# Fused attention and gated attention experts: the sum of the gate weights on GpSimd in place of VectorE, and the instructions in another order

## The chip, the cores and the metric

The kernel runs on one core of a Trainium2 chip. The metric is the device time of one launch in microseconds (us), the median over the runs of a kernel. The core's engines each work through a queue of their own, in order: TensorE (PE in the profile) for matrix products, ScalarE (ACT) for tanh and exp, VectorE (DVE), GpSimd (POOL), and SyncE (SP), which issues the transfers. PEld in the profile is TensorE's loading of weights, which may lie beside its products. Semaphores make one engine wait for another.

## The reference

Two layers in one launch. The first is attention with a soft cap, for 8 batches and 12 heads, 448 positions and 64 channels a head; the second is a gated attention with four experts, of which two count for each position.

```python
# layer 1: q, k, v of (8, 12, 448, 64)
scores = q @ k.T / sqrt(64)
scores = cap * tanh(scores / cap)          # cap = 30
attn = softmax(scores)
x = (attn @ v).transpose(0, 2, 1, 3).reshape(8, 448, 768)
# layer 2: w_gate (768, 4); wq, wk, wv (4, 768, 64); wo (4, 64, 768)
logits = x @ w_gate
topk = the two largest of four
w = softmax over the two chosen logits
for e in range(4):
    q, k, v = x @ wq[e], x @ wk[e], x @ wv[e]
    a = softmax(causal(q @ k.T / 8))
    ye = a @ v @ wo[e]
    out += (w of e where e is among the two, else 0) * ye
```

The output is (8, 448, 768) in float32.

## The kernel before, in words

**Layer 1** goes by pairs of heads: 48 pairs, six to a batch. For a pair, the float32 inputs are loaded by SyncE, cast to 16 bits on GpSimd (`cast`: k in L623, the zero-padded k in L628, q in L638, tails of k and v in L659 and L669, v in L664), transposed on TensorE (`tr`, L678 and L688) and copied out of PSUM on VectorE to `qk` (L707, L715). `fill` has TensorE write the scores into two PSUM regions, X and Y: `heads` (L752) and `tails` (L762), which are the last 64 keys. ScalarE makes three tanh of each pair (L805: Y1, X, Y2, where X holds 1344 columns and Y 896), and one exp of all of them (L817, 3136 columns for most pairs, 2240 for narrower ones). `pv` multiplies by v in two halves (L832 the tails, L839 the rest; a column of ones gives the sums). VectorE takes the reciprocal of the sums (`rca`, L860) and scales into `xk` (L863), which also sets the PSUM bank free. `xt` transposes `xk` on TensorE with a permutation (L878, `perm` and `pswap`), and VectorE copies that to `xT` (L887).

**Layer 2** follows a batch behind. `b_v` and `b_qk` project xT on TensorE (L947, L974); the logits of the gate come out of the same products as v. The gate is a chain of small tensors of 128 partitions, with four positions a partition:

- `b_gate` (GpSimd, L1014 to L1027): compares the logits pairwise and finds the ranks; `ms[0]`, `ms[1]` mark the first and the second expert
- `b_gate1` (GpSimd, L1036 to L1042): the difference of the two logits, in `g_e`
- `b_gexp` (GpSimd, L1048): its exponential, as a power of e
- `b_gate2`: 1 + e (VectorE, L1056), its reciprocal (VectorE, L1057), and on GpSimd e times that (L1058) and the two masked weights `mw` (L1060)

`b_mask` spreads the marks over the channels (`mB`, GpSimd, L1069), transposes them (L1080) and multiplies them into the queries (`qm`, VectorE, L1085 or L992). `b_score` (L1113) writes the scores of the chosen expert into the X region, in a batch twice, once for each rank; ScalarE's exp of them (L1122, 1024 columns) stands between the tanhs and exps of layer 1; `causal` zeroes what is masked, on GpSimd (L1132, L1139). `b_pv` multiplies by v (L1172), VectorE scales by the reciprocal of the sum and by `mw` (`oB`, L1187), `b_ot` adds the two ranks on GpSimd (`oS`, L1197) and transposes, `b_wo` multiplies by wo (L1234), in eight halves of 384 columns. `evac` (L381) copies each out of PSUM to `ob`, on VectorE or, near the end, on ScalarE, and SyncE stores it. The last batch is finished by `last2` and `last`.

**The order.** Every instruction is recorded as an operation with an occupancy and a latency, then `solve` builds the queues in one pass: of the operations of an engine that can start, it takes the one with the earliest due time. The activations of layer 1 and the exps of layer 2 on ScalarE are one fixed chain (`act(..., fixed=True)`). Due times are worked back from that chain. Operations with no score behind them get a due time by hand: that of the `xT` copy is `ACTS["Y1", p]` plus an offset, that of an `ob` copy another. What is taken depends on small numbers as well: a floor for due times, a bonus for operations in a PSUM group that is open, a tolerance for the start (`near`), a look ahead for operations marked `first`, and `SEEDS`, one number for each window of 4 us of planned time, which scatters the due times in it by up to half of `JIT` to either side. The costs in these calls (0.11, lat 0.17 and so on) steer the plan alone; the chip starts each instruction when its engine reaches it and its semaphores are there.

```python
d = u.due + lag if u.first or left < TAIL else max(u.due + lag, t0 + 1.12)
d -= 0.211 * (u.grp is not None and not u.opens and left >= TAIL)
k = SEEDS[int(t0 / 4.0)] if t0 < 4.0 * len(SEEDS) else 0
if k:
    d += ((u.idx * 40503 + k * 9973) % 1009 / 1009.0 - 0.5) * JIT
```

Of the kernel before, what the change touches and what calls it, by code (L numbers as in the profile page):

```python
# [11 lines left out]
ALU = mybir.AluOpType  # L12
# [4 lines left out]
SWITCH = 0.1  # L17
WARM = 5.5
TAIL = 4
LAND = 1.95  # L20
FLIGHT = 8
JIT = 0.549
SEEDS = (0, 277, 719, 88, 790, 157, 709, 606, 285, 730, 63, 826, 999, 577, 0, 998, 560, 424, 0, 0, 0, 0, 0, 618, 784, 951, 0, 460, 25, 911, 435, 331, 710, 235, 192, 243, 759, 815, 762, 59, 135, 842, 518, 725, 260, 0, 0, 0, 737, 833, 0, 852, 0, 951, 0, 877, 795, 0, 495, 199, 407, 374, 655, 0, 288, 645, 0, 0, 872, 410, 701, 204, 988, 494, 733, 571, 666, 645)
TWIRE = 0.1
BEGIN = {"POOL": 0.8, "DVE": 0.9, "SP": 0.8, "ACT": 0.8, "PE": 1.25}
NWARM = 9
# [25 lines left out]
class Graph:  # L52
# [79 lines left out]
    def solve(self, when, banks, lent):  # L132
        free = dict(BEGIN)
        sent = []
        ready = {}
        at = {}
        bank_at = {b: 0.0 for b in (*banks, *lent)}
        taken = {b: [o for o in self.ops if b in o.takes] for b in lent}
        for o in self.ops:
            o.nd = len(o.deps)  # L140
            if o.grp is not None:
                o.grp.bank = None
            if o.nd == 0:
                ready.setdefault(o.eng, []).append(o)
                at[o.idx] = 0.0
        order = []
        n = len(self.ops)
        left = sum(o.fixed for o in self.ops)
        half = 0
        lag = 0.0  # L150
        wire = 0.0

        def pick(o, t):
            best = None
            for b in o.grp.banks:
                s = max(t, bank_at[b])
                if s >= INF:
                    continue
                if b in taken and taken[b]:
                    continue  # L160
                if best is None or s < best[0]:
                    best = (s, b)
            return best or (INF, None)

        def est(o, e):
            t = max(free.get(e, 0.0), at[o.idx])
            if o.opens:
                t = pick(o, t)[0]
            for b in o.takes:
                t = max(t, bank_at[b])  # L170
            if (e == "SP" or o.wire) and len(sent) >= FLIGHT:
                t = max(t, sent[-FLIGHT])
            if e == "PE" and o.half != half:
                t = max(t, free.get(e, 0.0) + SWITCH)
            return t

        while len(order) < n:
            best = None
            for e, rs in ready.items():
                if not rs:  # L180
                    continue
                c = [(est(o, e), o) for o in rs if e == o.eng or not left]
                if not c:
                    continue
                t0 = min(x[0] for x in c)
                if t0 >= INF or (best is not None and t0 >= best[0]):
                    continue
                def rank(x):
                    u = x[1]
                    if u.name[:4] == "gexp":  # L190
                        return -INF, 0.0, 0
                    d = u.due + lag if u.first or left < TAIL else max(u.due + lag, t0 + 1.12)
                    d -= 0.211 * (u.grp is not None and not u.opens and left >= TAIL)
                    k = SEEDS[int(t0 / 4.0)] if t0 < 4.0 * len(SEEDS) else 0
                    if k:
                        d += ((u.idx * 40503 + k * 9973) % 1009 / 1009.0 - 0.5) * JIT
                    return d - 2.0 * (u.half == 1 and half == 1), u.due, u.idx

                near = t0 + (0.003 if left >= TAIL else SWITCH + 0.02)
                t, o = min((x for x in c if x[0] <= near), key=rank)  # L200
                early = e == "POOL" and t < HEAD
                if (e in ("PE", "DVE") or early) and not o.first:
                    for t2, u in c:
                        if u.first and u.due + lag < t + o.occ + 0.047 and t2 < t + (
                                o.occ if early else max(SWITCH + 0.01, min(o.occ, 0.25))):
                            t, o = t2, u
                            break
                if best is None or t < best[0]:
                    best = (t, e, o)
            assert best is not None, "stuck"  # L210
            t, e, o = best
            ready[o.eng].remove(o)
            if o.alt:
                ready[o.alt[0]].remove(o)
                if e != o.eng:
                    o.eng, o.occ, o.lat = o.alt
            left -= o.fixed
            o.start = t
            if e == "PE" and t < WARM:
                o.lat = 2.0 * o.base  # L220
                free[e] = t + 2.0 * o.base
                o.lat += 0.165
            else:
                free[e] = t + o.occ
            if o.wire:
                wire = max(wire, t + LAND) + o.wire
                o.lat = wire - t + 0.35
            if o.eng == "SP" or o.wire:
                sent.append(t + o.lat)
            if e == "PE":  # L230
                half = o.half
            if o.idx in when:
                lag = t - when[o.idx]
            if o.opens:
                b = pick(o, t)[1]
                o.grp.bank = b
                bank_at[b] = INF
            for b in o.takes:
                bank_at[b] = INF
                if b in taken:  # L240
                    taken[b].remove(o)
            if o.closes:
                bank_at[o.grp.bank] = t + o.lat + SEM
            for b in o.frees:
                bank_at[b] = t + o.lat + SEM
            order.append(o)
            for s, late in o.succ:
                at[s.idx] = max(at.get(s.idx, 0.0), t + self.gap(o, s, late))
                s.nd -= 1
                if s.nd == 0:  # L250
                    ready.setdefault(s.eng, []).append(s)
                    if s.alt:
                        ready.setdefault(s.alt[0], []).append(s)
        return order
# [19 lines left out]
def kernel(  # L274
# [13 lines left out]
    nc = tc.nc  # L288
# [12 lines left out]
    W1 = 320  # L301
# [4 lines left out]
    LB = B - 1  # L306
# [60 lines left out]
    def dve(occ, fn, r=(), w=(), grp=None, due=None, name="", lat=None):  # L367
        return G.op("DVE", occ, fn, r, w, occ + 0.085 if lat is None else lat, due, grp, name=name)
# [22 lines left out]
    def turned(n, dst, src, r, w, name, due=None):  # L391
# [58 lines left out]
    gt2 = [sb(f"gt2_{i}", sh, f32) for i, sh in enumerate(  # L450
        ([128, 1, E], [128, 1, E], [128, 1, E, E], [128, 2, 1, 1]))]
# [544 lines left out]
    def g_(b, fn, r, w, occ, lat):  # L996
        gp(occ, fn, r, [(b, y) for y in w], lat=lat, name=f"g{b}")
# [47 lines left out]
    def b_gexp(b, m=4):  # L1045
        x = b % 2
        e = g_e[x][:, 0:m]
        g_(b, lambda: nc.gpsimd.tensor_tensor(e, eul[:, 0:m], e, ALU.pow), [(b, "e"), "eul"],  # L1048
           ["e"], 1.05, 1.18)

    def b_gate2(b, m=4):
        x = b % 2
        V = nc.vector
        w = slice(0, m)
        e, w0 = g_e[x][:, w], g_w0[x][:, w]
        dve(0.11, lambda: V.tensor_scalar_add(w0, e, 1.0), [(b, "e")], [(b, "w0")], lat=0.17)  # L1056
        dve(0.1, lambda: V.reciprocal(w0, w0), [(b, "w0")], [(b, "w0")], lat=0.18)  # L1057
        g_(b, lambda: nc.gpsimd.tensor_tensor(e, e, w0, ALU.mult), [(b, "w0")], ["e"], 0.15, 0.28)  # L1058
        for s, t in ((0, w0), (1, e)):
            g_(b, lambda s=s, t=t: nc.gpsimd.tensor_tensor(  # L1060
                mw[s][x][:, w], ms[s][x][:, w], t.broadcast_to((128, m, E)), ALU.mult),
                [(b, f"ms{s}"), (b, "w0" if s == 0 else "e")], [f"mw{s}"], 0.17, 0.3)
# [404 lines left out]
    def last2(ref):  # L1467
# [63 lines left out]
        for e in range(E):  # L1531
            pe(0, lambda e=e: pv_(e), [("p2", e), "vL"] + [("vB", x, c) for c in range(3)],
               [("pvL", 3)], g, occ=0.12, name="pvL3")
        normed(3, g, view, ("pvL", 3), (gt2[0].rearrange("p o e -> p e o"), [(b, 2, "z"), (b, 2, "s")]),
               gt2[3][:, 1, 0], W1, (ref, 9.679))

# [12 lines left out]
    for p in range(NPV):  # L1551
# [13 lines left out]
        for what in order:  # L1565
            if what == "Y2" and p:
# [1 line left out]
                if p in exps:  # L1568
                    b_score(*exps[p])
                pv(p - 1)  # L1570
                xt(p - 1, (ACTS["Y1", p], 4.601))
                if p % HP == 0 and p < NP:
                    bb = p // HP - 1
                    b_v(bb, ACTS["Y1", p])
# [13 lines left out]
                if p in exps:  # L1588
                    bb, s = exps[p]
                    b_pv(bb, s)  # L1590
                    if s == 1:
                        b_ot(bb)
                        b_wo(bb, ACTS["Y1", p], *((14.83, 1.8) if bb < LB - 1 else (10.566, 0.5)))
            fill(p, what)
            tanh(p, what)
            if 0 < p < KEEP:
# [66 lines left out]
```

## Time and profile before

| | |
|---|---|
| median of 3 runs | 309.87 us (309.51 to 310.26) |
| the profiled execution | 309.16 us |
| its span in the profile | 307.4 us, 1.76 us less than its time |
| granted TensorE clock | 0.991 of full speed |
| busy: TensorE, ScalarE | 280.5 us (91%), 290.8 us (95%) |
| busy: VectorE, GpSimd | 216.0 us (70%), 181.4 us (59%) |
| HBM traffic over the span | 154 GB/s |

How to read it: busy time counts an instruction from its start to its end, and on ScalarE an activation that has been started but whose input isn't there yet counts as busy as well; the distance between the starts of two neighbours tells more than the duration. In rows of the timeline the columns are the start in us, the length in us, the engine, the line, the operation, what it writes and reads, shape and count; in square brackets stands idle time before it and what ended it. In rows of groups, behind the bar stand the busy time in us and the mean of one in ns, then idle time and its releaser. In rows of waits the columns are the sum in us, the number and the longest.

The chain of work that ended last runs over TensorE for 53% of the span, ScalarE for 30%, VectorE for 8% and GpSimd for 5%.

### The profile page before, as it was taken

How to read it: one execution, taken by the hardware profiler on the slowest of the kernel's cores; microseconds unless marked ns; L12 is line 12 of the kernel's file. 1: busy time of each engine (PE TensorE's matmuls, PEld its weight loads, DVE VectorE, ACT ScalarE, POOL GpSimd, SP SyncE). 2: the span in 40 equal slices, each digit the busy share in tenths (PEclk: the TensorE clock that was granted, in tenths of full speed). 3: DMA queues.
4: the chain of work that ended last, by engine and by line, in shares of the span. 5: the costliest groups of instructions: out<-in, count | busy, mean ns of one | idle time of the engine just before them, and what ended most of it. 6: DMA issues, size and time to landing. Idle time of an engine off the chain costs nothing.

```text
span 307.4 us, 8998 instructions
## 1 busy us (share of the span) xinstructions
PE 280.5 (91%) x3504; PEld 188.2 (61%) x3504; DVE 216.0 (70%) x660; ACT 290.8 (95%) x245; POOL 181.4 (59%) x502
## 2 busy tenths in 40 slices
PE   8787679999999999999999999999999989999992
PEld 4454446576655766667566676567665766577761
DVE  2363656477679867796866887787768765787882
ACT  3999999999999999999999999999999999999671
POOL 7883436499788572984649873946585413720320
PEclk9997999999999999999999999999999999999998
DMA  6997999899991798249975593186127600422136
GB/s 168 263 213 178 271 277 257 235 238 243 252 240 47 224 265 234 69 130 269 250 195 135 149 320 95 43 248 175 18 43 163 159 8 20 122 72 79 34 144 217
DMA packets 82075, 51.98 MB, mean 169 GB/s; under 512 B 42736, under 2 KB 78320, under 8 KB 82032
## 3 DMA queue, kind: packets, MB, share of 16 engines
q1 hardware_dynamic: 81728, 51.18, 63.7%
q8 instruction: 27, 0.44, 0.6%
q10 hardware_dynamic: 304, 0.23, 0.2%
q14 instruction: 16, 0.13, 0.1%
HBM read 36.19 MB, written 11.01 MB: 154 GB/s over the span
## 4 chain that ended last, share of the span: by engine, by line
PE 53%; ACT 30%; DVE 8%; POOL 5%; issue 2%; DMA 1%; DVEq 0%; ACTq 0%; POOLq 0%
ACT yp L805 15%; ACT yp L817 12%; PE A L974 7%; PE A L839 6%; PE Y L752 6%; PE A L947 4%; PE X L1113 4%; PE A L1234 4%; PE A L832 3%; PE A L1172 2%; PE A L878 2%; PE A L678 2%; DVE ob L381 2%; ACT pP L1122 2%; PE X L762 2%
## 5 line engine op out<-in xcount | busy, mean ns | idle before, releaser
L817 ACT ACTIVATE yp<-yp 128x3136 f16<-128x3136 f16 (+4 forms) x51 | 139.8, 2744 | 0.0
L805 ACT ACTIVATE yp<-Y 128x896 f16<-128x896 f32 (+2 forms) x100 | 96.2, 962 | 1.6 <-PE Y L752 1.6
L805 ACT ACTIVATE yp<-X 128x1344 f16<-128x1344 f32 (+2 forms) x50 | 65.9, 1318 | 0.1
L839 PE MATMUL A<-v,yp 128*128 128x65 f16 x1116 | 55.9, 194 | 0.0
L839 PEld LDWEIGHTS <-yp 128*128 128x128 f16 x1116 | 49.0, 98 | 4.9 <-issue 2.9
L832 PE MATMUL A<-vtz,yp 128*128 128x130 f16 x186 | 41.5, 223 | 10.0 <-ACT yp L817 5.4
L863 DVE TENSOR_TENSOR xk<-A,rca 128x256 f16<-128x256 f32 (+1 forms) x96 | 39.7, 415 | 2.8
L860 DVE RECIPROCAL rca<-A 128x4 f32<-128x4 f32 (+1 forms) x96 | 17.2, 179 | 25.6 <-PE A L839 24.1
L638 POOL CAST q<-qf 112x512 f16<-112x512 f32 x44 | 26.6, 613 | 13.6 <-DMA qf<-in_q_dram 6.6
L664 POOL CAST v<-vf 128x384 f16<-128x384 f32 x48 | 24.4, 514 | 11.2 <-PE A L839 7.1
L381 DVE COPY ob<-A 128x384 f32<-128x384 f32 (+1 forms) x52 | 28.1, 552 | 3.9 <-PE A L1234 2.8
L832 PEld LDWEIGHTS <-yp 128*128 128x128 f16 x186 | 18.1, 97 | 20.0 <-ACT yp L817 11.2
L1187 DVE SCALAR_TENSOR_TENSOR oB<-A,rcb,mw 128x256 f16<-128x256 f32 x54 | 25.3, 479 | 1.4
L715 DVE COPY qk<-A 128x960 f16<-128x960 f16 x33 | 21.0, 653 | 7.2 <-PE A L678 6.7
L752 PE MATMUL Y<-qk 64*128 64x448 f16 x136 | 24.9, 361 | 0.8 <-ACT yp L805 0.4
L1234 PE MATMUL A<-wo,oT 128*128 128x384 f16 x108 | 24.3, 326 | 0.8 <-DVE ob L381 0.3
L1197 POOL TENSOR_TENSOR oS<-oB,oB 128x512 f16<-128x512 f16 x14 | 16.1, 1153 | 14.4 <-DVE oB L1187 10.4
L1172 PE MATMUL A<-vB,pP 128*128 128x260 f16 x135 | 22.8, 274 | 1.0 <-DVE qk L715 0.7
L947 PE MATMUL A<-wvg,xT 128*128 128x260 f16 x168 | 23.0, 274 | 0.2
L678 PE MATMUL A<-ident,q 112*128 112x112 f16 x192 | 20.2, 212 | 2.3 <-DVE q L638 0.8
L623 POOL CAST k<-kf 128x384 f16<-128x384 f32 x33 | 16.6, 512 | 9.7 <-DMA kf<-in_k_dram 6.0
L887 DVE COPY xT<-A 128x448 f16<-128x448 f16 (+1 forms) x48 | 18.0, 377 | 4.8 <-PE A L878 4.5
(231 smaller groups left out, 587.3 us busy)
## 6 DMA issues: line engine op xcount, KB each, us to landing
qf<-in_q_dram SPq DMA_DIRECT2D x23, 448.0 KB, 6.3
kf<-in_k_dram SPq DMA_DIRECT2D x23, 384.0 KB, 5.7
vf<-in_v_dram SPq DMA_DIRECT2D x23, 384.0 KB, 5.1
out_dram<-ob SPq DMA_DIRECT2D x21, 384.0 KB, 3.3
ktf<-in_k_dram SPq DMA_DIRECT2D x46, 32.0 KB, 5.0
vtf<-in_v_dram SPq DMA_DIRECT2D x46, 32.0 KB, 4.5
out_dram<-ob SPq DMA_DIRECT2D x6, 192.0 KB, 3.3
ob<-in_moe_wv_dram SPq DMA_DIRECT2D x2, 384.0 KB, 5.0
```

What stands on the lines that cost most here:

```text
L381: (nc.scalar.copy if o.eng == "ACT" else nc.vector.tensor_copy)(dst(), src())
L638: e(q16[i], qf[s][:, h].rearrange("p h (c d) -> p c h d", c=QC))
L678: nc.tensor.transpose(ps[:, 0:S].rearrange("m (g c t) -> m c g t", c=QC, t=16)[:, c], q16[i][:, c, :, :].rearrange("p h d -> p (h d)"), id ...
L752: nc.tensor.matmul(dst[:, g, o], kT[r, 128 * (c + 1) : 128 * (c + 2)], t[r, qs], start=True, stop=True,)
L805: ACTS[what, p] = act(c_act(n * (b - a)), lambda: nc.scalar.activation(y[:, a:b, 0:n], src[:, 0 : b - a, 0:n], AF.Tanh, scale=isc / capf), ...
L817: act(c_act(n * (b - a), False), lambda a=a, b=b, n=n: nc.scalar.activation(y[:, a:b, 0:n], y[:, a:b, 0:n], AF.Exp, scale=capf), ks, ks, f ...
L832: nc.tensor.matmul(ps[:, n, :, :], y[:, 2, w : w + 128], vtz[u], start=(n == 0), stop=False, skip_group_check=True,)
L839: nc.tensor.matmul(ps[:, n, h, :], y[:, SLOT[c][h], w : w + 128], v16[u][:, h, c, :], start=False, stop=(c == 2), skip_group_check=True,)
L863: dve(c_dve(128 * m), lambda g=g, i=i, rc=rc, m=m: nc.vector.tensor_tensor(xk[p % NXK][:, 2 * i : 2 * i + m, :, :], view(g)[:, 0:m, :, 0:D ...
L947: nc.tensor.matmul(bank(g)[:, 0 : E * Dh + E], xT[x][:, j, w : w + 128], wvg[:, j, :], start=(j == 0), stop=(j == NDC - 1),)
L1172: nc.tensor.matmul(bank(g)[:, 0 : E * (Dh + 1)], pB[pi][:, o : o + 128], vB[x][:, c, :, :], start=(t == 0), stop=(t == len(cs) - 1),)
L1234: nc.tensor.matmul(bank(g)[:, 0 : D // 2], oT[x][:, n // 2, r, n % 2, :], wo2[r][:, c0:c1], start=(r == 0), stop=(r == 1),)
```

## The change

The addition of 1 to e leaves `b_gate2`, where VectorE did it (`V.tensor_scalar_add`, L1056). In `b_gexp` GpSimd does the same addition behind the power, with an instruction of its own (`tensor_scalar` with `ALU.add`). VectorE's reciprocal then reads what GpSimd wrote. There is one such addition a batch in seven of the eight batches. Beside that, 50 of the 78 numbers in `SEEDS` differ, as do the floor for due times, the bonus, the tolerance, the look ahead, and three offsets of due times. No other operation is added or removed, but the queues stand in another order, and near the end some copies out of PSUM are made by the other of ScalarE and VectorE. In the kernel after, the lines behind `b_gexp` have numbers higher by one.

```diff
--- before.py
+++ after.py
@@ -20,7 +20,7 @@
 LAND = 1.95
 FLIGHT = 8
 JIT = 0.549
-SEEDS = (0, 277, 719, 88, 790, 157, 709, 606, 285, 730, 63, 826, 999, 577, 0, 998,
...
+SEEDS = (0, 0, 719, 88, 733, 597, 709, 0, 78, 526, 63, 826, 0, 653, 0, 128,
...
 TWIRE = 0.1
 BEGIN = {"POOL": 0.8, "DVE": 0.9, "SP": 0.8, "ACT": 0.8, "PE": 1.25}
 NWARM = 9
@@ -189,19 +189,19 @@
                     u = x[1]
                     if u.name[:4] == "gexp":
                         return -INF, 0.0, 0
-                    d = u.due + lag if u.first or left < TAIL else max(u.due + lag, t0 + 1.12)
-                    d -= 0.211 * (u.grp is not None and not u.opens and left >= TAIL)
+                    d = u.due + lag if u.first or left < TAIL else max(u.due + lag, t0 + 1.124)
+                    d -= 0.191 * (u.grp is not None and not u.opens and left >= TAIL)
                     k = SEEDS[int(t0 / 4.0)] if t0 < 4.0 * len(SEEDS) else 0
                     if k:
                         d += ((u.idx * 40503 + k * 9973) % 1009 / 1009.0 - 0.5) * JIT
                     return d - 2.0 * (u.half == 1 and half == 1), u.due, u.idx
 
-                near = t0 + (0.003 if left >= TAIL else SWITCH + 0.02)
+                near = t0 + (0.012 if left >= TAIL else SWITCH + 0.02)
                 t, o = min((x for x in c if x[0] <= near), key=rank)
                 early = e == "POOL" and t < HEAD
                 if (e in ("PE", "DVE") or early) and not o.first:
                     for t2, u in c:
-                        if u.first and u.due + lag < t + o.occ + 0.047 and t2 < t + (
+                        if u.first and u.due + lag < t + o.occ + 0.0 and t2 < t + (
                                 o.occ if early else max(SWITCH + 0.01, min(o.occ, 0.25))):
                             t, o = t2, u
                             break
@@ -1047,13 +1047,14 @@
         e = g_e[x][:, 0:m]
         g_(b, lambda: nc.gpsimd.tensor_tensor(e, eul[:, 0:m], e, ALU.pow), [(b, "e"), "eul"],
            ["e"], 1.05, 1.18)
+        g_(b, lambda: nc.gpsimd.tensor_scalar(g_w0[x][:, 0:m], e, 1.0, None, ALU.add), [(b, "e")],
+           ["w0"], 0.19, 0.34)
 
     def b_gate2(b, m=4):
         x = b % 2
         V = nc.vector
         w = slice(0, m)
         e, w0 = g_e[x][:, w], g_w0[x][:, w]
-        dve(0.11, lambda: V.tensor_scalar_add(w0, e, 1.0), [(b, "e")], [(b, "w0")], lat=0.17)
         dve(0.1, lambda: V.reciprocal(w0, w0), [(b, "w0")], [(b, "w0")], lat=0.18)
         g_(b, lambda: nc.gpsimd.tensor_tensor(e, e, w0, ALU.mult), [(b, "w0")], ["e"], 0.15, 0.28)
         for s, t in ((0, w0), (1, e)):
@@ -1532,7 +1533,7 @@
             pe(0, lambda e=e: pv_(e), [("p2", e), "vL"] + [("vB", x, c) for c in range(3)],
                [("pvL", 3)], g, occ=0.12, name="pvL3")
         normed(3, g, view, ("pvL", 3), (gt2[0].rearrange("p o e -> p e o"), [(b, 2, "z"), (b, 2, "s")]),
-               gt2[3][:, 1, 0], W1, (ref, 9.679))
+               gt2[3][:, 1, 0], W1, (ref, 9.667))
 
 
 
@@ -1568,7 +1569,7 @@
                 if p in exps:
                     b_score(*exps[p])
                 pv(p - 1)
-                xt(p - 1, (ACTS["Y1", p], 4.601))
+                xt(p - 1, (ACTS["Y1", p], 4.556))
                 if p % HP == 0 and p < NP:
                     bb = p // HP - 1
                     b_v(bb, ACTS["Y1", p])
@@ -1590,7 +1591,7 @@
                     b_pv(bb, s)
                     if s == 1:
                         b_ot(bb)
-                        b_wo(bb, ACTS["Y1", p], *((14.83, 1.8) if bb < LB - 1 else (10.566, 0.5)))
+                        b_wo(bb, ACTS["Y1", p], *((14.809, 1.8) if bb < LB - 1 else (10.566, 0.5)))
             fill(p, what)
             tanh(p, what)
             if 0 < p < KEEP:
```

(Of `SEEDS` only the beginning is shown.)

## The prediction

> **What bounds the kernel now.** I read the busy times first, then ScalarE's timeline, then the engines around the places where ScalarE is late.
>
> ```profile
> span 307.4 us, 8998 instructions
> PE 280.5 (91%) x3504; PEld 188.2 (61%) x3504; DVE 216.0 (70%) x660; ACT 290.8 (95%) x245; POOL 181.4 (59%) x502
> ```
>
> ScalarE (ACT) is busy for 95% of the span, TensorE (PE) for 91%. VectorE (DVE), from which work is taken, and GpSimd (POOL), which receives it, stand at 70% and 59%. So the microseconds that change engines are not worth their length. What counts is whether ScalarE, whose program is one fixed chain of tanh and exp, gets each tile of scores when its turn comes.
>
> Busy time hides that: an activation that starts early and waits for its scores is shown as a longer one. I therefore read distances from start to start. Four rows give the undisturbed steps, and one later pair that of the narrower exp:
>
> ```profile
> 188.91 1.37 ACT L805 ACTIVATE yp<-X 128x1344 f16<-128x1344 f32 x1
> 190.08 1.01 ACT L805 ACTIVATE yp<-Y 128x896 f16<-128x896 f32 x1
> 190.87 2.91 ACT L817 ACTIVATE yp<-yp 128x3136 f16<-128x3136 f16 x1
> 193.58 1.01 ACT L805 ACTIVATE yp<-Y 128x896 f16<-128x896 f32 x1
> ...
> 265.77 2.24 ACT L817 ACTIVATE yp<-yp 128x2240 f16<-128x2240 f16 x1
> 267.73 0.88 ACT L805 ACTIVATE yp<-Y 128x640 f16<-128x640 f32 x1
> ```
>
> A tanh of X takes 1.17 us (190.08 − 188.91), one of Y 0.79, an exp of 3136 columns 2.71, an exp of 2240 columns 1.96. The steps that are longer than that are these:
>
> ```profile
> 70.46 1.11 ACT L805 ACTIVATE yp<-Y 128x896 f16<-128x896 f32 x1
> 71.42 1.34 ACT L805 ACTIVATE yp<-X 128x1344 f16<-128x1344 f32 x1
> ...
> 140.74 1.08 ACT L805 ACTIVATE yp<-Y 128x896 f16<-128x896 f32 x1
> 141.78 1.29 ACT L805 ACTIVATE yp<-X 128x1344 f16<-128x1344 f32 x1
> ...
> 172.13 2.93 ACT L817 ACTIVATE yp<-yp 128x3136 f16<-128x3136 f16 x1
> 175.35 1.02 ACT L1122 ACTIVATE pP<-X 128x1024 f16<-128x1024 f32 x1 [0.28 <-PE X L1113]
> ...
> 207.29 2.98 ACT L817 ACTIVATE yp<-yp 128x3136 f16<-128x3136 f16 x1
> 210.26 1.02 ACT L1122 ACTIVATE pP<-X 128x1024 f16<-128x1024 f32 x1
> ...
> 269.74 2.27 ACT L817 ACTIVATE yp<-yp 128x2240 f16<-128x2240 f16 x1
> 272.49 1.02 ACT L1122 ACTIVATE pP<-X 128x1024 f16<-128x1024 f32 x1 [0.48 <-PE X L1113]
> ```
>
> The excess is 0.17 us before 71.42, 0.25 before 141.78, 0.51 before 175.35 (3.22 − 2.71), 0.26 before 210.26 and 0.79 before 272.49 (2.75 − 1.96). Together that is 1.98 us in which ScalarE stood behind scores, and where a releaser is named it is a TensorE score group (L1113). A few more such places, each smaller than the largest of these, have equal work ahead of them in both orders. I leave them unchanged. After the last activations TensorE sets the pace alone:
>
> ```profile
> 286.80:296.00 9.20, 9.20 (x113) 6.44 (x111) 7.80 (x31) 6.01 (x16) 4.19 (x9) 1.00 0.24 72
> ```
>
> Columns: length, then busy time of PE, weight load, DVE, ACT, POOL. TensorE is busy for all 9.20 us. So the change can act by two ways: what stands ahead of late scores in TensorE's queue, and what waits for VectorE on the way to them.
>
> **The change part by part.** First the moved operation.
>
> ```profile
> L1056 DVE TENSOR_SCALAR g_w<-g_e 128x4 f32<-128x4 f32 x7 | 2.7, 387 | 1.2 <-POOL g_e L1048 1.1
> L1056 DVE TENSOR_SCALAR g_w<-g_e x7: 140/316/820, 70.2 to 266.7; 128x4 f32<-128x4 f32 x7
> L1027 POOL TENSOR_SCALAR ms<-g_r 128x16 f32<-128x16 f32 x14 | 3.3, 253 | 0.2
> 70.25 0.51 POOL L664 CAST v<-vf 128x384 f16<-128x384 f32 x1
> ```
>
> VectorE loses seven additions, 2.7 us in all, between 140 and 820 ns each. GpSimd gets seven. The trace has no GpSimd addition with a constant on 128x4; the nearest row is its comparison with a constant on 128x16, 253 ns, so I take 7 × 0.25 = 1.8 us. The bounds are 0.2 us (nothing but the short VectorE price) and 0.8 us each. On both engines this lies beside other work: there is room of 30% and 41%. The sum takes 0 for it where no score waits, and the one place where a score does wait is worked out below. Without cover it would cost at most 0.25 − 0.14 = 0.11 us per batch.
>
> The longest addition, at 70.2, runs beside GpSimd's cast of v at 70.25, which keeps its 0.51 us; the shortest is 140 ns for equal data. The Trainium skill (GPSIMD Engine Reference, section 8, Key points) says that GpSimd shares its SBUF interfaces with VectorE and that they contend when VectorE runs in a 2-port mode; the stretch of 140 to 820 ns beside a cast agrees with it, and by this rule the move takes the stretch away for good. The same section speaks against the change: it calls VectorE structurally about twice as fast for elementwise work, so that an estimate by this page of the Trainium skill is 2 × 140 = 280 ns on GpSimd, 7 × 0.28 = 2.0 us where the row gives 1.8. The trace agrees with the rule for the short additions, not for the mean, since 387 ns is more than 253.
>
> Now the places, by the order of instructions of the changed kernel as built, set against that of before. ScalarE's order is the same up to the tail. TensorE has the same 3504 matmuls, and the groups of scores shift by less than 1 us of queued work against the rest.
>
> *At 272.49.* The work ahead of the last score group is this:
>
> ```profile
> 270.36 0.23 PE L832 MATMUL A<-vtz,yp 128*128 128x130 f16 x1
> ...
> 270.85 0.81 PE L1234 MATMUL A<-wo,oT 128*128 128x384 f16 x4
> 271.50 0.50 PE L1113 MATMUL X<-qm,kB 128*128 128x128 f16 x6
> ```
>
> Two halves of a p·v product take 0.49 us (270.85 − 270.36), four wo matmuls 0.65. In the changed order one half (0.25) and two wo matmuls (0.33) stay ahead: −(0.49 + 0.65 − 0.25 − 0.33) = −0.56, of a stall of 0.79. Next late would be the rest of the score group itself, 0.23.
>
> *At 175.35.* VectorE's addition is on the path here:
>
> ```profile
> 172.98 0.56 DVE L1056 TENSOR_SCALAR g_w<-g_e 128x4 f32<-128x4 f32 x1
> 173.45 0.41 DVE L863 TENSOR_TENSOR xk<-A,rca 128x256 f16<-128x256 f32 x1
> ...
> 173.16 0.49 PE L1234 MATMUL A<-wo,oT 128*128 128x384 f16 x2
> 173.92 0.48 PE L1234 MATMUL A<-wo,oT 128*128 128x384 f16 x2 [0.27 <-DVE xk L863]
> 174.24 0.33 PE L878 MATMUL A<-perm,xk 128*128 128x128 f16 x3
> 174.41 0.22 PE L878 MATMUL A<-pswap,xk 128*128 128x128 f16 x1
> 174.46 0.79 PE L1113 MATMUL X<-qm,kB 128*128 128x128 f16 x14
> ```
>
> The addition holds VectorE 0.47 us ahead of xk, and xk frees the bank for the wo matmuls at 173.92. The pair before them needs 0.33, so TensorE stood 0.43 (173.92 − 173.16 − 0.33). Without the addition that wait goes (−0.43). But in the changed order two more wo pairs stand ahead of the last score matmuls (+0.65), while a p·v half (−0.25) and the transposes of xk (four, 174.46 − 174.24 = −0.22) come behind: +0.18. Net −0.25, with ends −0.5 (the whole stall) and +0.3 (the wait stays, and the work comes on top).
>
> *At 210.26.* The rows are on VectorE:
>
> ```profile
> 207.03 0.56 DVE L381 COPY ob<-A 64x384 f32<-64x384 f32 x1
> 207.62 0.39 DVE L707 COPY qk<-A 128x448 f16<-128x448 f16 x1
> ```
>
> The copy of tail queries and keys feeds a score matmul, and stood 0.59 us behind a copy of output. In the changed order it goes ahead of that. The stall of 0.26 goes (−0.26; if another matmul is late then, +0.2 at the other end).
>
> *At 141.78.* One wo pair (0.33) and three transposes of xk (174.41 − 174.24 = 0.17) leave the queue ahead of the X scores: more than the stall of 0.25, of which I take −0.20, ends −0.25 and +0.1.
>
> *At 71.42* three p·v halves stand ahead instead of two (+0.25), and three copies of queries and keys follow each other on VectorE; part of it is slack, so +0.1 (−0.17 to +0.4). *At 84.6*, one matmul of 260 columns more: 0.65 / 4 × 260 / 384 = +0.11.
>
> Sum: −0.56 − 0.25 − 0.26 − 0.20 + 0.10 + 0.11 = −1.06. A chain that runs earlier by a microsecond meets loads, casts and copies that did not hold it before. For new stalls I add one of ordinary size, the mean of the four smaller ones above, (1.98 − 0.79) / 4 = +0.3; ends 0 and +1.2 (four of them). The tail has the same TensorE work in both, 0 (±0.5). What is left is −0.8.
>
> The profiled execution took 309.16 us, its span and 1.76 around it. The median of the runs is 309.87, 0.71 above. −0.8 gives 308.4 for a profiled execution and **309.1 us** for the median. No change means within 0.2%, 0.62 us, about what a measurement of this kernel can tell.
>
> **The rivals.**
>
> *The gains are filled again.* The stalls that go are replaced: the new order has other late tiles, and 1 us comes back. For it: TensorE is at 91% over the whole span, so a score group that moves up pushes another piece back. Against it: ScalarE's excess is concentrated in few places, and these are the ones that the order relieves. 309.8 us.
>
> *VectorE's reciprocal waits for GpSimd; slower.* The addition on GpSimd does not follow the power directly. In the changed order casts stand between in five of seven batches: in the first a cast of q and one of ktz.
>
> ```profile
> DVE g_w L1056 <- POOL g_e L1048: 1.1, 1, 1.1
> L638 POOL CAST q<-qf 112x512 f16<-112x512 f32 x44 | 26.6, 613 | 13.6 <-DMA qf<-in_q_dram 6.6 <-PE A L678 6.6
> L659 POOL CAST ktz<-ktf 128x128 f16<-128x128 f32 x34 | 9.6, 292 | 1.0 <-DMA ktf<-in_k_dram 0.9
> ```
>
> VectorE waited for the power only once, 1.1 us. The reciprocal now becomes ready up to 0.61 + 0.29 + 0.25 = 1.15 us behind the power's end. VectorE runs in order: behind a waiting reciprocal stand rca, xk and the copies of queries and keys, and for these wait the wo matmuls and the scores. At 173 a hold of 0.47 on VectorE made a TensorE wait of 0.43 and belonged to a stall of 0.51. A wait of the full 1.15 is 0.7 more than that hold; two such waits (1.4) and the loss of the credit at 175.35 (0.25) turn −0.8 into +0.85: 310.7 us. It decides where less than 1.15 us (0.25 where no cast stands between) lie between the power's end and the reciprocal's turn. Against it: the power is placed about 1 us earlier in the changed order, and GpSimd has 41% of room.
>
> *Deeper gain.* VectorE is relieved in all seven batches (2.7 us) and xk with its transposes moves up nearly everywhere; the 1.98 goes but for 0.4, the ends of the terms above, without give-back: −1.6, 308.3 us. For it: the long additions, 820 ns. Against it: only the addition at 172.98 is seen on a path. By the contention rule of the Trainium skill named above, this is the case if GpSimd's casts wait for no VectorE addition any more; no row here shows a cast that was held.
>
> *A worse tail.* From 286.8 on TensorE is full, and the copies of output are split over ScalarE and VectorE in another order with due times moved by some hundredths. If two banks there come free late by one copy each (0.56, the row of 207.03), TensorE waits 1.1: with half of the gains kept, 309.87 − 0.4 + 1.1 = 310.6 us. For it: no cover there at all, PE 9.20 of 9.20. Against it: the same work in nearly the same order.
>
> **How the numbers follow.** The forecast, −0.6 to −1.2, gets 0.36 (own range 308.6 to 309.25); deeper 0.11; filled again 0.27; the reciprocal's wait 0.17; the tail 0.09. Faster by over 0.2% is forecast and deeper, 0.47; no change 0.27; slower 0.26. The range must leave out no more than 2 in 10: from 308.3, the middle of the deeper case, to 310.7, that of the slower one, which leaves out half of each of them, 0.14, and a little of the tail.
>
> **What would show it.** In the changed kernel's profile: the starts before the gate exps near 175 and 272 come 3.0 and 2.2 us after the exp ahead of them instead of 3.22 and 2.75; the step before 210 is 2.71. GpSimd's new addition takes 0.2 to 0.3 us. The waits of VectorE show g_w behind GpSimd for under 1 us in all; over 2 us there, and late scores behind it, and the slower rival holds. TensorE's work is the same, so a span that changes without a change in ScalarE's steps up to 286 would have it from the tail, and my sum would be wrong in its place.

## The result, and the profile after

The changed kernel takes 311.21 us (median of 22 runs, 308.78 to 313.10), the kernel before 309.69 us in the same number of runs (309.08 to 310.76). The ratio is 1.0045, with a 95% interval of 1.0029 to 1.0061: slower by nearly half a per cent, outside the range that was given. The runs of the changed kernel also scatter more than twice as far. Ratios here and below are over undisturbed runs of both kernels and need not be the quotient of the medians.

The profiled execution took 311.22 us. The first lines of its page, and the chain that ended last:

```profile
span 309.5 us, 8994 instructions
PE 281.9 (91%) x3504; PEld 189.6 (61%) x3504; DVE 212.8 (69%) x652; ACT 291.2 (94%) x246; POOL 183.3 (59%) x509
...
PE 51%; ACT 15%; POOL 11%; DVE 9%; DMA 8%; issue 4%; SPq 1%; POOLq 0%; DVEq 0%
```

VectorE lost 3.2 us of work (2.7 of it the additions) and GpSimd gained 1.9, about as planned, and the span is 2.1 us longer. The last line tells where to look: in the chain, ScalarE's share fell from 30% to 15%, GpSimd's rose from 5% to 11%, and DMA's from 1% to 8%. ScalarE's timeline shows the places (start, length, and in brackets idle time and its releaser):

```profile
9.18 0.93 ACT L805 ACTIVATE yp<-Y 128x896 f16<-128x896 f32 x1
10.70 1.29 ACT L805 ACTIVATE yp<-X 128x1344 f16<-128x1344 f32 x1 [0.60 <-PE X L752]
...
172.24 2.93 ACT L817 ACTIVATE yp<-yp 128x3136 f16<-128x3136 f16 x1
175.01 1.07 ACT L1123 ACTIVATE pP<-X 128x1024 f16<-128x1024 f32 x1
...
206.95 3.04 ACT L817 ACTIVATE yp<-yp 128x3136 f16<-128x3136 f16 x1
209.90 1.02 ACT L1123 ACTIVATE pP<-X 128x1024 f16<-128x1024 f32 x1
...
239.87 1.46 ACT L805 ACTIVATE yp<-X 128x1344 f16<-128x1344 f32 x1
243.22 0.92 ACT L805 ACTIVATE yp<-Y 128x896 f16<-128x896 f32 x1 [1.90 <-PE Y L752]
...
271.61 2.22 ACT L817 ACTIVATE yp<-yp 128x2240 f16<-128x2240 f16 x1
274.88 1.02 ACT L1123 ACTIVATE pP<-X 128x1024 f16<-128x1024 f32 x1 [1.04 <-PE X L1114]
```

Excess over the undisturbed steps, worked out from starts over the whole chain in both traces, in us (what is small in both is left out):

| stretch | before | after | difference |
|---|---|---|---|
| to 33 (first pairs) | 0.34 | 0.72 | +0.39 |
| 70 to 150 | 1.31 | 0.82 | −0.49 |
| 172 and 207 (gate exps) | 0.77 | 0.31 | −0.46 |
| 240 | 0 | 2.18 | +2.18 |
| 248 to 253 | 0.16 | 0.19 | +0.03 |
| 272 | 0.79 | 1.30 | +0.52 |
| sum of the rows | 3.37 | 5.52 | +2.17 |

(Entries are rounded one by one.) ScalarE's first tanh starts 0.17 us later in the changed kernel (7.20 against 7.03) and its last exp of layer 1 2.41 us later (286.48 against 284.07), where the spans differ by 2.1: the tail is some 0.3 us shorter. From 70 to 207 the new order is better by 0.95 us, about twice what the prediction's terms for these places add up to (−0.50); two places near the end and one at the start take more than that back. This is one execution of each kernel, and others of the changed kernel can lose their time elsewhere.

**What is late at 240 and 272.** On VectorE, in the changed kernel, the products that put the masks into the queries wait for a transfer:

```profile
236.67 0.62 DVE L992 TENSOR_TENSOR qm<-A,mT 128x448 f16<-128x448 f32 x1 [1.39 <-DMA mT<-mB]
...
271.37 0.62 DVE L992 TENSOR_TENSOR qm<-A,mT 128x448 f16<-128x448 f32 x1 [3.09 <-DMA mT<-mB]
...
DMA to landing us min/median/max: 2.7/3.6/4.6
```

For the last three of the seven batches the masks are transposed by a DMA (`turned`, L393), not by TensorE. Before, VectorE never waited for one, and the same view gave for all six:

```profile
DMA to landing us min/median/max: 2.7/2.8/2.8
```

Two things differ here, and at 240 a third. First, GpSimd makes the masks of batch 5 later; before stands in the first fence, after in the second:

```profile
227.94 2.28 POOL L1069 CAST mB<-ms 128x512 f16<-128x512 f32 x4
230.18 1.15 POOL L1197 TENSOR_TENSOR oS<-oB,oB 128x512 f16<-128x512 f16 x1
```

```profile
226.70 1.15 POOL L1198 TENSOR_TENSOR oS<-oB,oB 128x512 f16<-128x512 f16 x1
...
228.08 0.51 POOL L664 CAST v<-vf 128x384 f16<-128x384 f32 x1
...
229.69 2.28 POOL L1070 CAST mB<-ms 128x512 f16<-128x512 f32 x4
```

The sum `oS` of the batch before it and two casts went ahead of the masks: 1.75 us. Second, the later transposes meet something. The DMA view between the first issue and the last landing of batch 5's masks, before and after (queue and kind: packets, MB, share of the 16 DMA engines' time; then issues with median us to landing):

```profile
q1 hardware_dynamic: 2138, 0.53, 58.8%
...
mT<-mB SPq DMA_TRANSPOSE x2, 2.7
```

```profile
q1 hardware_dynamic: 2261, 0.93, 90.9%
q8 instruction: 1, 0.02, 1.6%
...
mT<-mB SPq DMA_TRANSPOSE x2, 3.6
```

The one packet on q8 is 16 KB of instructions. There are 27 of them in a run, one for about every 256 of TensorE's instructions (3504 products and 3504 weight loads). The packet near 233 starts in both kernels at the same place of TensorE's program (5298 of its recorded instructions have started), the one near 267 at 6081 and 6082. Before, the data of the masks' transposes were through 0.1 to 0.9 us ahead of the next packet. After, the packets at the two places took 1.47 and 1.69 us, and packets of 256 bytes of the transposes that were under way took up to 2.0 us in place of 0.02.

Third, at 240, TensorE's granted clock (columns: stretch, its length, busy us of PE, PEld, DVE, ACT, POOL, then granted clock, DMA share, GB/s):

```profile
234.20:237.60 3.40, 1.80 (x27) 1.14 (x26) 2.01 (x5) 3.40 (x4) 0.98 (x3) 0.99 0.68 190
237.60:241.00 3.40, 3.40 (x37) 2.23 (x34) 2.09 (x8) 3.40 (x3) 1.01 (x4) 0.50 0.22 42
```

TensorE, behind VectorE, was busy for 1.80 of 3.40 us, and got half the clock for the next 3.4 us, with a full queue. The loss does not need this: two other runs of the changed kernel, whose granted clock was 1.000 on average, took 310.91 and 310.97 us, still over 1 us more than the median of the kernel before.

**At the start** TensorE's queue has transposes of k of the third and fourth pair ahead of scores of the second, and waits there for GpSimd's cast of a load:

```profile
10.02 0.34 PE L688 MATMUL A<-ident,k 128*128 128x128 f16 x3 [0.27 <-POOL k L623]
10.30 0.36 PE L752 MATMUL X<-qk 64*128 64x448 f16 x2
```

### The profile page after: what moved, and what is told of

The parts are those of the page before. It is cut to its first block, busy times and chain, and to the rows that moved or that the text cites. A ratio compares the mean times of both kernels' runs of the same rounds, so it can differ in the third digit from the quotient of the medians.

```text
span 309.5 us, 8994 instructions
## 1 busy us (share of the span) xinstructions
PE 281.9 (91%) x3504; PEld 189.6 (61%) x3504; DVE 212.8 (69%) x652; ACT 291.2 (94%) x246; POOL 183.3 (59%) x509
## 4 chain that ended last, share of the span: by engine, by line
PE 51%; ACT 15%; POOL 11%; DVE 9%; DMA 8%; issue 4%; SPq 1%; POOLq 0%; DVEq 0%
ACT yp L805 8%; ACT yp L817 7%; PE A L839 6%; PE Y L752 6%; PE A L974 5%; PE A L947 5%; PE A L1235 4%; PE A L832 3%; DMA mT<-mB 3%; PE A L1173 3%; PE X L1114 3%; DMA ktf<-in_k_dram 2%; PE X L752 2%; POOL mB L1070 2%; PE A L678 2%
## 5 line engine op out<-in xcount | busy, mean ns | idle before, releaser
L805 ACT ACTIVATE yp<-Y 128x896 f16<-128x896 f32 (+2 forms) x100 | 98.0, 980 | 3.5 <-PE Y L752 3.4
L805 ACT ACTIVATE yp<-X 128x1344 f16<-128x1344 f32 (+2 forms) x50 | 67.0, 1339 | 0.7 <-PE X L752 0.6
L839 PE MATMUL A<-v,yp 128*128 128x65 f16 x1116 | 56.8, 194 | 0.0
L381 DVE COPY ob<-A 128x384 f32<-128x384 f32 (+1 forms) x51 | 27.3, 554 | 5.0 <-PE A L1235 4.4
L1235 PE MATMUL A<-wo,oT 128*128 128x384 f16 x108 | 25.1, 330 | 0.3
```

The source lines that it names most:

```text
L381: (nc.scalar.copy if o.eng == "ACT" else nc.vector.tensor_copy)(dst(), src())
L805: ACTS[what, p] = act(c_act(n * (b - a)), lambda: nc.scalar.activation(y[:, a:b, 0:n], src[:, 0 : b - a, 0:n], AF.Tanh, scale=isc / capf), ...
L839: nc.tensor.matmul(ps[:, n, h, :], y[:, SLOT[c][h], w : w + 128], v16[u][:, h, c, :], start=False, stop=(c == 2), skip_group_check=True,)
L1235: nc.tensor.matmul(bank(g)[:, 0 : D // 2], oT[x][:, n // 2, r, n % 2, :], wo2[r][:, c0:c1], start=(r == 0), stop=(r == 1),)
```

## The experiments

Two theories were set against each other. By the theory of the fetches, the new order brings the transposes of the masks under TensorE's instruction packets, and the moved addition is free; by the theory of the reciprocal, the slower rival of the prediction, VectorE's reciprocal waits for GpSimd's addition. Later ones are named where they come up. All kernels below keep an order of instructions exactly as the plan of before or of after had it, and change only what is named; the result is always timed against the kernel before.

**The two halves of the change.** `add_alone`: order of before, GpSimd adds behind the power.

```diff
-        g_(b, lambda: nc.gpsimd.tensor_tensor(e, eul[:, 0:m], e, ALU.pow), ...
+        g_(b, lambda: (nc.gpsimd.tensor_tensor(e, eul[:, 0:m], e, ALU.pow),
+                       nc.gpsimd.tensor_scalar(g_w0[x][:, 0:m], e, 1.0, None, ALU.add)), ...
-        dve(0.11, lambda: V.tensor_scalar_add(w0, e, 1.0), ...
+        dve(0.11, lambda: None, ...
```

> The order of before, instruction by instruction, with the seven additions made by GpSimd right behind the power instead of by VectorE. Theory of the fetches (the new order brings the mask transposes of batches 5 and 6 onto TensorE's 16 KB instruction fetches, and VectorE waits for the masks; the addition itself is free): 309.4 to 309.9 us, within 0.3 of before, no wait of VectorE for the power over 0.5 us. Theory of the reciprocal (VectorE waits for GpSimd's addition and everything behind it is late): slower by 0.5 us or more, with waits of VectorE's g_w behind GpSimd over 1 us.

Measured 309.35 us, ratio 0.9987 (0.9978 to 0.9996): the moved addition is a small gain. ScalarE's step into 175:

```profile
172.72 2.93 ACT L817 ACTIVATE yp<-yp 128x3136 f16<-128x3136 f16 x1
175.49 1.08 ACT L1123 ACTIVATE pP<-X 128x1024 f16<-128x1024 f32 x1
```

2.77 us instead of 3.22: the stall that the prediction laid to VectorE's addition is gone (−0.45) with nothing else moved. One part of the expectation failed: near 267 VectorE waited 1.43 us for GpSimd's addition, as the theory of the reciprocal had it, but the next gate exp was no later for it (step 2.74, before 2.75).

`order_alone`: order of after, VectorE adds ahead of its reciprocal.

```diff
-        g_(b, lambda: nc.gpsimd.tensor_scalar(g_w0[x][:, 0:m], e, 1.0, None, ALU.add), ...
+        g_(b, lambda: None, ...
-        dve(0.1, lambda: V.reciprocal(w0, w0), ...
+        dve(0.1, lambda: (V.tensor_scalar_add(w0, e, 1.0), V.reciprocal(w0, w0)), ...
```

> The order of after, instruction by instruction, with the additions back on VectorE, each right ahead of its reciprocal. Theory of the fetches: as slow as after, 310.8 to 311.7 us, with the same two waits of VectorE for the transposed masks near 235 and 270. Theory of the reciprocal: back to 309.7 us or less.

Measured 311.67 us, ratio 1.0045 (1.0028 to 1.0061), the same ratio as after: the loss is the order's. In its profiled run the step at 240 was longer by 0.76 us, not 2.18, and the clock stayed up, although TensorE's busy time falls to 1.91 of 3.40 in one stretch ahead (a stretch of the same length that starts 0.7 us earlier, at 234.9, has 2.37):

```profile
235.60:239.00 3.40, 1.91 (x30) 1.21 (x27) 1.98 (x5) 3.40 (x4) 1.06 (x3) 1.00 1.19 229
239.00:242.40 3.40, 3.24 (x46) 2.00 (x43) 3.30 (x12) 3.40 (x3) 1.34 (x5) 1.00 0.07 13
```

**The fetches moved against the work.** Warm-up products of TensorE, which compute nothing that is used, are joined or split, so that every later 16 KB packet comes later or earlier.

```diff
 # after_fetch_later: 28 short warm-up products -> 7 of 512 columns
+        ji = i - NWARM
+        few = None if ji < 0 or ji >= 28 else 512 if ji % 4 == 3 else 0
 # before_fetch_early, after_fetch_60: products of 512 columns in 2 or 3 parts
-                    pe(512, lambda g=g: nc.tensor.matmul(bank(g)[:, 0:512], ...
+                    pe(512, lambda g=g: [nc.tensor.matmul(bank(g)[:, 256 * i : 256 * (i + 1)], ...
+                       ) for i in range(2)],
```

> The order of before with the addition on VectorE, but each of the 21 warm-up products of 512 columns in the first pairs split into two of 256, 42 TensorE instructions more, so that every later fetch comes 42 instructions earlier against the work and falls on the transposes of the masks, which in before end 0.2 to 0.9 us ahead of it. Theory of the fetches: transposes land after 4 us or more in at least two of the three batches that use them, VectorE waits for them, 310.5 to 312.5 us. Theory of the reciprocal: no change, 309.7.

Measured 310.81 us, ratio 1.0034 (1.0016 to 1.0053), as that theory had it. Landing, VectorE's waits, and a step of ScalarE that before took 1.17 and here takes 1.77:

```profile
DMA to landing us min/median/max: 2.7/4.0/4.4
...
DVE qm L992 <- DMA mT<-mB: 1.9, 2, 1.3
...
241.17 1.29 ACT L805 ACTIVATE yp<-X 128x1344 f16<-128x1344 f32 x1
242.94 0.92 ACT L805 ACTIVATE yp<-Y 128x896 f16<-128x896 f32 x1 [0.48 <-PE Y L752]
```

So the packets alone, with the order of before, make the kernel slower. The 42 added instructions are not what costs: in the first 35 us the excess is 0.14, in before 0.28, and the new excess lies at 235 (0.45), 241 (0.60) and 270 (0.22), behind the masks. (The first tanh starts 0.53 us later, but that start lies anywhere from 7.03 to 7.84 us in the twelve profiled kernels.)

> The order of after with the addition on GpSimd, but 28 of the 30 short warm-up products of 128 columns ahead of the first scores are joined four to one (7 of 512 columns), so that TensorE has 21 products, 42 instructions, less before everything else, and every later fetch of its instructions comes 42 instructions later against the work, 1.5 to 2 us. Theory of the fetches: the mask transposes of batches 5 and 6 land 2.7 to 2.9 us after their issue instead of 4.5, VectorE's waits for them fall from 4.5 us to under 1.5, 309.2 to 310.0 us. Theory of the reciprocal: no change, 311.2.

A miss: 314.01 us, ratio 1.0108 (1.0076 to 1.0140); the runs lie between 310.57 and 315.28, and the profiled one is the longest. The packet that came near 221 in after now came at 224.4, onto two other transposes:

```profile
q8 instruction: 1, 0.02, 1.9%
...
kd<-kz SPq DMA_TRANSPOSE x1, 5.0
oT<-oS SPq DMA_TRANSPOSE x1, 4.1
...
POOL kz L628 <- DMA kd<-kz: 3.7, 1, 3.7
```

GpSimd stood 3.7 us for the buffer (1.7 in after), everything behind it was later, and the masks met the packets again. The masks' part is the expected mechanism at another place: one shift moves every packet. That the packet at 224.4 made `kd` late is argued: transfers of `kd` took 3.2 to 5.3 us without a packet beside them as well.

> The order of after with 15 of the 21 warm-up products of 512 columns split into three of 170, so that TensorE's instruction fetches come 60 instructions earlier against the work, some 2 us, ahead of the transposes of the masks of batches 5 and 6 and ahead of the transfers near 221, and right behind those of batch 4. Theory of the fetches: all six mask transposes land within 3 us, no wait of VectorE for them over 0.5 us, 309.0 to 310.0 us. Theory of the masks alone (their place in GpSimd's queue costs the time, the fetch nothing): VectorE still waits over 0.5 us for batch 5, 310.7 to 311.5.

Measured 310.14 us, ratio 1.0013 (0.9996 to 1.0031), 1.1 us below after, a little over what was expected. The packet lay clear ahead of the masks of batch 6, and from 0.6 us ahead of the first issue of batch 5 to 0.9 behind it. The step at 240 that took 3.35 us takes 1.17, and the one at 272 that took 3.27 takes 2.17:

```profile
241.42 1.44 ACT L805 ACTIVATE yp<-X 128x1344 f16<-128x1344 f32 x1
242.59 1.08 ACT L805 ACTIVATE yp<-Y 128x896 f16<-128x896 f32 x1
...
270.95 2.27 ACT L817 ACTIVATE yp<-yp 128x2240 f16<-128x2240 f16 x1
273.12 1.02 ACT L1123 ACTIVATE pP<-X 128x1024 f16<-128x1024 f32 x1
```

GpSimd's queue was untouched, so the masks' place there did not suffice for the loss. Half of the expectation failed: a packet caught the masks of batch 4 (198.5, landing 4.0), with stalls of 1.1 us there (0.2 in after), and VectorE still waited 1.83 us in batch 5 (landing 3.6 and 3.1), but not long enough to make scores late.

**The masks put back.** `after_masks_early`: order of after, with `oS`, two casts, the transfer of `oS` and a store behind batch 5's masks (`delay` puts named operations, and what hangs on them, behind another one).

```diff
+    order = delay(order, (2032, 2391, 2392, 2039), 1976)
     for o in order:
         o.fn()
```

> The order of after, with one thing put back: GpSimd's second sum oS of batch 4, two casts of v, the transposing transfer of that sum and one store stand behind the masks of batch 5 and their transposes, instead of ahead of them, about as in before. TensorE's, VectorE's and ScalarE's queues are untouched. Theory of the masks (they come too late to the transposing transfer, which then meets TensorE's instruction fetch): the transposes of batch 5 are issued 1.7 us earlier, land under 3 us later and ahead of the fetch near 233, VectorE's wait of 1.39 us there and ScalarE's stall of 2.2 near 240 go; batch 6 stays as it is: 309.0 to 309.9 us. Theory of many small delays (the order is worse in general, by TensorE's own queue): within 0.5 of after, 311.

Measured 309.92 us, ratio 1.0009 (0.9992 to 1.0026), 1.3 us below after. Masks and clock:

```profile
229.12 2.28 POOL L1070 CAST mB<-ms 128x512 f16<-128x512 f32 x4
...
234.20:237.60 3.40, 2.93 (x44) 2.05 (x42) 2.50 (x6) 3.40 (x5) 2.03 (x4) 1.00 0.89 168
237.60:241.00 3.40, 3.24 (x44) 2.04 (x42) 3.00 (x11) 3.40 (x4) 1.33 (x5) 1.00 0.70 179
```

The packet comes where it came, the transposes are through, the clock stays at 1.00, and the step at 240 has no excess. So the stall at 240 needed both, late masks and the packet; taking away either removes it. (The edit moves a store and a transfer as well, `after_fetch_60` nothing but the packets.) Batch 6 stays as it was: a packet beside its masks, landing 4.0, and an excess of 0.64 at 272.

**The start.** `after_start`: TensorE's transposes of k behind the second pair's scores, `delay(order, (139, 171), 147)`.

> The order of after, but in TensorE's queue the transposes of k of the third and fourth pair (L688) stand behind the X and Y scores of the second pair near 10 us, as in before, instead of ahead of them; nothing else moves. Theory of the start (TensorE waits there for GpSimd's cast of a load, and the scores behind it are late): ScalarE's step from 9.2 us is 0.85 again instead of 1.5 to 2.4, and the kernel 0.5 to 1.0 us faster than after: 310.2 to 310.8 us. Theory that the delay there is caught up behind: no change, 311.2.

Measured 309.70 us, ratio 1.0007 (0.9988 to 1.0026), 1.5 below after, more than expected. The runs lie between 308.0 and 311.2. The step from 9.65 is 0.85 us again, but in the profiled run, one of the longest (311.20), the wait came back one pair on, behind other loads:

```profile
16.40 0.92 ACT L805 ACTIVATE yp<-Y 128x896 f16<-128x896 f32 x1 [1.09 <-PE Y L752]
```

`after_masks_start` has both edits.

> The order of after with two things put back: the masks of batch 5 and their transposes ahead of the sum, the casts and the store, and the transposes of k of the third and fourth pair behind the second pair's scores. If the two places carry the whole loss and the other terms of the prediction hold (the stalls near 141, 175 and 101 are gone in the new order): 308.9 to 309.3 us, below before and not above the kernel with the addition alone moved. If the new order has a further loss: 309.7 or more.

Measured 309.11 us, ratio 0.9975 (0.9961 to 0.9989): faster than before, and 2.1 us below after, where the two edits alone gave 1.3 and 1.5. The new order has no further loss of size.

**The term of 272.49, alone.** `add_scores_early`: `add_alone`, with what stood ahead of the last scores of batch 6 put behind them, `delay(order, (2458, 2459, 2361, 2363, 2465), 2502)`.

> The order of before with the addition on GpSimd right behind the power, and one more edit: ahead of the last five score products of the first rank of batch 6 (near 270), two halves of p.v, the two pairs of wo and one set of transposes of xk are put behind them, with their copies. The prediction's term of -0.56 for the stall of 0.79 at 272.49, tested alone: 308.6 to 309.0 us, 0.4 to 0.7 below the kernel with the addition on GpSimd alone. If what is put off is missed elsewhere at once: 309.3.

Measured 309.31 us, ratio 0.9990 (0.9978 to 1.0003): no gain over 309.35.

```profile
269.80 2.27 ACT L817 ACTIVATE yp<-yp 128x2240 f16<-128x2240 f16 x1
271.76 1.22 ACT L1123 ACTIVATE pP<-X 128x1024 f16<-128x1024 f32 x1
272.66 0.91 ACT L805 ACTIVATE yp<-Y 128x640 f16<-128x640 f32 x1
274.49 1.13 ACT L805 ACTIVATE yp<-X 128x1152 f16<-128x1152 f32 x1 [0.91 <-PE X L752]
```

The gate exp is on time (1.96), and the X scores two steps on are late by more (1.83 − 0.58 = 1.25). TensorE had to do that work ahead of one or the other.

**A version that beats both.** `after_loads`: `after_masks_start` with SyncE's loads of the third pair's k and q and the first v in the order of before.

```diff
+    want = (128, 54, 125, 55, 126, 56, 127)
+    slots = [i for i, o in enumerate(order) if o.idx in want]
```

> The kernel with both places of the new order put back (masks of batch 5 early, the transposes of k behind the second pair's scores), and SyncE's first loads in the order of before: the third pair's k and q no longer all ahead of the first v. If those loads made the difference between its own quick runs (307.8 to 308.5) and the others (309.0 to 309.8): median 308.0 to 308.7. If the spread comes from the transposes of batch 6 and the clock alone: 309.1, no change.

Measured 308.45 us, ratio 0.9958 (0.9944 to 0.9972; 5 runs): the lowest median of all, and what the first case expected. Its interval overlaps that of `after_masks_start`, so that the loads made the difference is likely, not shown. In its profiled run (309.08) VectorE still waited 3.4 us for batch 6's masks, with a landing of 4.9: what is left there was not tried.

## Why the prediction was wrong, point by point

- **The moved operation** was priced right: 237 ns each on GpSimd against the 253 taken, hidden; the row of all seven in the changed kernel:

```profile
L1050 POOL TENSOR_SCALAR g_w<-g_e 128x4 f32<-128x4 f32 x7 | 1.7, 237 | 0.2
```

- **The reciprocal's rival**, on which the slower side rested, was rejected rightly: VectorE's waits in after have no row for g_w, and `add_alone` is faster than before. The slower case came by another way.
- **At 175.35**, −0.25 forecast, −0.45 measured (2.77 against 3.22). The addition alone, in the order of before, gives as much; the new order with the addition on VectorE (`order_alone`) gives −0.24. The term was mis-sized: the wo pairs that were to cost +0.18 cost nothing.
- **At 141.78**, −0.20 forecast, −0.23 measured. **At 71.42** and **84.6**, +0.10 and +0.11 forecast, −0.09 and +0.27 measured. **At 101.4**, left unchanged, 0.36 went; it went in `add_alone` as well, where the order is that of before, so "equal work ahead of them" was not enough to leave a place out.
- **At 210.26**, −0.26 forecast, −0.02 measured (2.95). The copy did go ahead (206.60 against 207.62), but TensorE's queue ran without a gap from 207.3 to the last score products in both kernels: they stood behind wo pairs and p·v halves, not behind the copy.
- **At 272.49**, −0.56 forecast, +0.52 measured. This is the step that failed: work ahead in TensorE's queue was counted, and the other input of the same products, `qm`, was not followed back to the masks, GpSimd's queue and the transfer. The count itself was right: where the masks of batch 6 came in time in this order (`after_fetch_60`), the step is 2.17, an excess of 0.21 where the prediction had 0.23. Moved so in the order of before, the same work brought nothing, since the next scores paid (`add_scores_early`).
- **At 240** the prediction had no term, and it is the same failed step: masks that came late. **New stalls**, +0.3 with ends 0 and +1.2, were sized as "one of ordinary size"; this one was 2.18, with the lower clock. The same place had 0.76 and 0.85 in profiled runs that kept the clock (`order_alone`, `after_start`). How much of the difference the clock made was not separated. Beyond what was forecast, 240 and 272 are 1.9 and 1.1 us, about the whole miss of 2.9 between the −0.8 forecast and the +2.1 of the profiled spans; what was better in between and worse at the start is of a smaller size.
- **"The groups of scores shift by less than 1 us of queued work"** was not enough. It counts TensorE's work ahead, not what a product there waits for: at 10 us a transpose that needs a cast of a load, worth +0.67 at that step here; in the profiled runs of four other kernels with this start the excess is 1.0 to 1.6.
- **The tail**, 0 forecast (±0.5): right, about −0.3.

Without the two misplaced groups the forecast order gives 309.11 us. That the number is the forecast one is in part chance, since single terms were off in both directions.

## What to carry to other kernels

When a schedule is changed, follow every input of a late product back through all queues, and list the transfers whose landing had little slack: here a margin of 0.1 to 0.9 us ahead of an instruction fetch was worth 1.2 us in 310 (`before_fetch_early`). Test an order against an edit by freezing the order, since both change together whenever a planner is run again. When TensorE falls idle for part of a few microseconds, its clock may be lower afterwards, so a wait can cost more than its length.

## What the runs showed of the hardware

**Instruction fetches and transposing transfers.** TensorE's 16 KB packets took 0.9 to 2.6 us. The twelve profiled executions hold 72 transposes of masks. The 26 with a packet that started between 0.6 us ahead of the issue and 2.25 us behind it landed after 3.6 to 4.9 us; of the other 46 all but two (3.1 and 4.7) landed after 2.7 to 2.9. That packet and transpose share one of the DMA engines is argued from the packets' lengths, not shown by itself. The Trainium skill (Runtime: NRT & Kernel Launch, Instruction fetch mechanics) says that instructions are refilled in blocks of 16 KiB, 256 instructions, by a DMA queue of the engine's own, and calls the cost mostly hidden. The size and the rhythm agree with the trace. On TensorE no cost is seen (in after it was busy for all 2.40 us from 232.0 to 234.4, across the start of the packet at 233.34); for the transposes beside it the cost was not hidden.

**The clock.** The granted clock fell to 0.50 for 3.4 us behind a stretch of 3.4 us in which TensorE was busy for 1.80, its longest single wait in it 1.12. Busy time alone does not tell when: in `add_alone` it fell behind a stretch with 1.95 (11.8 to 15.2), in `order_alone` it stayed at 1.00 behind one with 1.79 (36.9 to 40.3). The Trainium skill (TensorE: Matmul & The Clock Gate, Part 1, What's actually happening) tells of a free-running window of about 3.4 us and of a clock that is either half or full. Both agree with the trace; a window that is idle as a whole, if that is what the section's table means by an idle window, was not needed here.
